# Identity products on an idle TensorE, pooled attention by two head pairs, and output tiles in a shared ring

## The chip, the cores and the metric

The kernel runs on one core of a Trainium2 chip. The metric is the device time of one execution in microseconds (us), the median of several executions. TensorE (PE) multiplies matrices into PSUM, its weight loads are counted as PEld; VectorE (DVE), ScalarE (ACT) and GpSimd (POOL) work element by element, POOL on SBUF only; SyncE (SP) issues the transfers. All engines take their queues in order.

## The reference, cut to what matters

Four sequences of 576 tokens, 8 heads of 64. Two attentions are added, one over means of four tokens, one over a band of seven, and a bilinear MLP follows.

```python
q_d = q.reshape(B, H, Sd, 4, D).mean(axis=3)        # the same for k and v, Sd = 144
out_d = sm_attn(q_d, k_d, v_d)                       # softmax(scale q k^T) v
out_up = np.repeat(out_d, 4, axis=2)
mask = np.abs(pos[:, None] - pos[None, :]) < 4
scores = np.where(mask, scale * np.matmul(q, k.transpose(0, 1, 3, 2)), -1000000000.0)
out_local = np.matmul(softmax(scores), v)
x = (out_up + out_local).transpose(0, 2, 1, 3).reshape(2304, 512)
result = ((x @ w_a) * (x @ w_b)) @ w_out             # w_a, w_b: 512 x 1536, w_out: 1536 x 512
```

## The kernel before, in words

**Tiling.** The 2304 tokens are cut in 9 units of 256 for the attentions and in 6 token tiles of 384 for the MLP. Heads go in 4 pairs (`NP`). The MLP splits each operand into a high and a low part (`xh`, `xl`; `gh`, `gl`; two halves of each `w`) and forms three products per pair of operands (`products`, lines 754 to 759). Per token tile there are 12 steps `f`, each with a product group `psa`, a group `psb` and a group `po`, 12 matmuls of 384 columns each, so 36 groups per token tile (`m_up`, `m_down`, lines 761 to 788). Afterwards `m_store` (lines 790 to 805) copies four PSUM banks to SBUF tiles `o` and stores them. For the first five token tiles the `o` tiles have a tag of their own with one buffer; for the last one they go to the tag `prod`, a ring of 3 buffers that the banded attention's products (`pr`, `av`) and the dense blocks' loads (`qk`, `vb`) use too.

**Weights.** 18 transfers of 1 MB bring the weights as 8-byte words; `w_pair` (lines 392 to 425) takes them apart: scalings and shifts on `ws`, a joining step to `wd`, the high part `w`, the low part `w`.

**Pooled attention.** For unit `u` and head pair `p`: `g_load` loads, `g_pools` sums four tokens (`g_sum`, lines 623 to 631, on POOL in three additions or on DVE in one reduction) into `qd`, `kd` and `vd`; `g_scores` (lines 649 to 667) multiplies into the bank `gs`, takes the negative maximum (`gnb`), exponentiates on ACT into `ge` with the sum in `gsm`; `g_norm` (669 to 674) divides; `g_turn` (676 to 685) transposes twice into `gt` and copies back; `g_out` (687 to 702) multiplies into `go` and copies to `xd`. `qd` has two buffers, one for odd and one for even pairs, and the banks come from the tag `misc` with two buffers. A unit that crosses two sequences has its products in two parts.

**Local attention.** The first two units (512 tokens, 8 blocks of 64) do it densely on PE (`d_steps`, lines 521 to 586: `ds` scores with a bf16 product of `band` that puts the mask in, `dt` transposes, `do` outputs, `add` adds the pooled part and splits into `xh`, `xl`). Blocks 0 to 5 make up the first token tile. The other seven units do it with products on POOL or DVE (`pr`, `av`), reductions on DVE (`sc`, `xloc`) and transposes on PE (`xp`); `x_steps` (lines 720 to 749) adds the pooled part and splits.

**What sets the order.** Nothing is issued as the functions are called: each call records a step with the engines that could do it, a cost for each, a rank and its predecessors. `Steps.order` (lines 202 to 268) then plans all engines by a list schedule in which the earliest possible step of the smallest rank goes first, `run_pe` (270 to 281) models PE's clock, and `emit` issues the result, which is fixed from then on. Ranks come from due times: `pooled`, `dense`, `banded` (lines 813 to 841) and the weights' line (857) take them from the constants of lines 46 to 62 (`PLAN`, `LEAD`, `LOAD_LEAD`, `W_STREAM`); the constants named `..._ON_DVE` are penalties for doing a step on DVE rather than on POOL or ACT. The prices of a step on PE stand in its call (0.174 us for an MLP product, 0.11 for a transpose of the pooled part, 0.06 for a dense output product).

Of the kernel before, what the change touches and what calls it, by code (L numbers as in the profile page):

```python
# [7 lines left out]
F32 = mybir.dt.float32  # L8
# [6 lines left out]
ALU = mybir.AluOpType  # L15
# [4 lines left out]
P = 128  # L20
# [37 lines left out]
LEAD = {"L": 2.852, "G": -12.651, "D0": -16.602, "D1": -2.24, "G0": 8.66}  # L58
PLAN = {"g0": -58.062, "g0s": 1.06, "g1": -27.374, "g1s": 4.983, "g2": 20.007, "g2s": 1.791,
        "d0": -31.319, "d0s": 5.13, "a0": -17.442, "a1": -7.9, "d1": 3.872, "d1s": 4.978, "t2": 19.293,  # L60
        "c2": 0.454, "t3": 34.824, "c3": 0.572, "t4": 57.774, "c4": 0.45, "t": -35.57, "c": 0.155}
LOAD_LEAD = {"L": -3.486, "G": 5.822, "D0": 13.151, "D1": -3.246, "G0": 20.908}
# [64 lines left out]
class Steps:  # L127
# [11 lines left out]
    def __init__(self, engines):  # L139
        self.engines, self.steps, self.tags = engines, [], {}  # L140
        self.rank, self.open = 0.0, None

# [59 lines left out]
    def order(self, window):  # L202
# [17 lines left out]
        done, duty = [], {}  # L220
        while True:
# [24 lines left out]
            if best is None:  # L246
                break
            at, e, (_, _, s, cost, _) = best
# [18 lines left out]
        assert len(done) == len(self.steps)  # L267
# [24 lines left out]
def tile_pooled_and_banded_attention__then__bilinear_mlp(  # L292
# [228 lines left out]
    def d_steps(b):  # L521
# [55 lines left out]
        def add():  # L577

            assert ready.count(u) == NP
# [53 lines left out]
    def g_pools(u, p):  # L633
# [8 lines left out]
        if b is not None:  # L642
            kd_t[b, p] = kd = tile_([P, NG], F32, "kd", f"kd{b}_{p}", bufs=5)
            vd_t[b, p] = vd = tile_([KC, 2, P], F32, "vd", f"vd{b}_{p}", bufs=5)
# [4 lines left out]
    def g_scores(u, p):  # L649
        qd = qd_t[p % 2].rearrange("p g j -> p (g j)")  # L650
        nb = tile_([P, 1], F32, "gnb", f"gnb{u}_{p}", bufs=2)
        tl = tile_([P, 2 * P], F32, "ge", f"ge{u}_{p}")
        e = tl[:, :NG]
        sm = tile_([P, 1], F32, "gsm", f"gsm{u}_{p}", bufs=2)
        ps = misc(f"gs{u}_{p}")[:, :NG]
# [11 lines left out]
        g_st[u, p] = (e, sm, tl)  # L667

    def g_norm(u, p):
        e, sm, _ = g_st[u, p]  # L670
        dve("tensor_scalar", 1, sm, sm, 1e-9, 4.0, op0=ALU.add, op1=ALU.mult)
        steps.steps[-1].shared = False
        dve("reciprocal", 1, sm, sm)
        act(NG, e, e, AF.Copy, scale=sm)

    def g_turn(u, p):
        e, _, tl = g_st[u, p]
        ps = misc(f"gt{u}_{p}")[:KC, : 2 * P]
# [6 lines left out]
        g_st[u, p] = pt.rearrange("p (c g j) -> p c g j", c=2, j=2)  # L685

    def g_out(u, p):
        pt = g_st.pop((u, p))
        ps = misc(f"go{u}_{p}")[:, :GU]
        steps.group()  # L690
        for n, (b, c0, c1) in enumerate(spans(u)):
            for c in range(2):

                for j in range(2):
                    rows = slice(j * D, (j + 1) * D)
                    mm(0.08, ps[rows, c0:c1], vd_t[b, p][:, c, rows], pt[:, c, c0:c1, j],
                       n == 0 and c == 0, c == 1, (c1 - c0) * KC / 6e2 / P)
# [3 lines left out]
        copy(GU, xd[u].part(p)[:, p], ps)  # L701
# [18 lines left out]
    def x_steps(u, th):  # L720
# [11 lines left out]
        def add():  # L732
            assert ready.count(u) == NP
# [56 lines left out]
    def m_store(m):  # L790
# [3 lines left out]
        for i, ps in enumerate(m_st["out"]):  # L794
            o = tile_([P, MT], F32, *(("prod", f"o{m}_{i}", 3) if m == NM - 1 else ("o", f"o{m}_{i}")))
# [70 lines left out]
    load(170, band, band_d)  # L866
    load(128, ident, ident_d)
    for t in qd_t:
# [4 lines left out]
    for m in range(NM):  # L873
# [6 lines left out]
        for s, (kind, f) in enumerate(slots):  # L880
# [4 lines left out]
            else:  # L885
                m_up(m, f, kind)
        steps.rank = m * 36 + 36
# [105 lines left out]
```

## Time and profile before

| | |
|---|---|
| median of 3 executions | 587.44 us (587.41 to 588.31) |
| the profiled execution | 586.48 us |
| its span, first to last instruction | 584.3 us |
| busy of the span: PE, DVE, ACT, POOL | 546.1, 407.0, 189.4, 277.2 us |
| chain that ended last, by engine | PE 87%, DVE 6%, DMA 3%, ACT 2% |
| mean granted TensorE clock | 0.998 |

How to read it: one execution was taken by the hardware profiler. An engine's busy time is the union of its instructions; a matmul's end is modelled and overlaps the next one's start, so the distance from start to start says more of PE than a duration. The chain follows back from the last instruction to what released each step. The granted clock is the share of TensorE's 2.4 GHz that the profiler's records show. In a row, `out<-in` names the tiles written and read, `x12` counts instructions, and `[0.92 <-DVE xl]` is the engine's idle time before the row and what ended it. All instructions stand at line 288, where `emit` issues them, so rows are told apart by tile.

### The profile page before, as it was taken

The page shows a single profiled execution, that of the slowest core. Times are in us where ns is not written, and L with a number is a line of the kernel's source. Part 1 is how long each engine was busy: PE and PEld are TensorE (multiplying, and loading weights), DVE is VectorE, ACT ScalarE, POOL GpSimd, SP SyncE. Part 2 cuts the span into 40 slices and gives each one's busy share as a digit, 9 for nine tenths or more (in the row PEclk, how much of TensorE's full clock was granted, in tenths as well). Part 3 has the DMA queues.
Part 4 walks back from the last instruction along what each step waited for, and adds up shares of the span by engine and source line. Part 5 has one row for each costly group of instructions (what it writes and reads, how often), then busy time and mean ns, then how long its engine had stood idle before and what let it go on. Part 6 is the DMA issues. An engine that isn't in the chain of part 4 may idle for free.

```text
span 584.3 us, 9037 instructions
## 1 busy us (share of the span) xinstructions
PE 546.1 (93%) x3432; PEld 517.9 (89%) x3432; DVE 407.0 (70%) x717; ACT 189.4 (32%) x464; POOL 277.2 (47%) x254
## 2 busy tenths in 40 slices
PE   2687599999989999999999999999999999999995
PEld 1565499889989999989999999999999999999995
DVE  5599999588989998888798897993787351221121
ACT  1599996222233123243212222231132111111111
POOL 4420421578867868769868696794154000000000
PEclk9999999999999999999999999999999999999999
DMA  8999990242133223422222432201110000000001
GB/s 235 343 360 375 345 320 2 85 151 72 72 110 102 76 79 102 145 87 103 70 82 64 153 96 78 82 32 50 33 42 13 2 1 0 28 28 0 1 1 54
DMA packets 22219, 59.51 MB, mean 102 GB/s; under 512 B 2544, under 2 KB 9072, under 8 KB 19872
## 3 DMA queue, kind: packets, MB, share of 16 engines
q1 hardware_dynamic: 22176, 58.93, 29.9%
q8 instruction: 27, 0.44, 0.3%
q14 instruction: 16, 0.13, 0.1%
HBM read 54.20 MB, written 4.72 MB: 101 GB/s over the span
## 4 chain that ended last, share of the span: by engine, by line
PE 87%; DVE 6%; DMA 3%; ACT 2%; issue 1%; SPq 0%; POOL 0%; ACTq 0%; DVEq 0%; POOLq 0%
PE psa L288 26%; PE psb L288 26%; PE po L288 24%; PE gs L288 3%; PE go L288 3%; DMA qk<-in_qk_dram 2%; PE ds L288 1%; PE gt L288 1%; DVE w L288 1%; DVE xloc L288 1%; PE dt L288 1%; PE do L288 1%; PE xp L288 1%; DVE xp L288 1%; DMA kv<-in_kqg_dram 1%
## 5 line engine op out<-in xcount | busy, mean ns | idle before, releaser
L288 PE MATMUL psa<-xh,w 128*128 128x384 f32 x576 | 162.5, 343 | 0.3 <-ACT xh L288 0.3
L288 PE MATMUL psb<-xh,w 128*128 128x384 f32 x576 | 160.7, 339 | 0.4 <-ACT a L288 0.4
L288 PE MATMUL po<-gh,w 128*128 128x384 f32 x576 | 160.0, 339 | 0.0
L288 POOL TENSOR_TENSOR pr<-q,k 128x896 f32<-128x896 f32 x50 | 106.3, 2146 | 7.4 <-DVE sc L288 2.3
L288 PEld LDWEIGHTS psa<-xh,w 128*128 128x128 f32 x576 | 106.2, 190 | 1.8 <-issue 1.1
L288 PEld LDWEIGHTS psb<-xh,w 128*128 128x128 f32 x576 | 105.4, 188 | 1.9 <-ACT a L288 0.6
L288 POOL TENSOR_TENSOR av<-v,sc 128x896 f32<-128x896 f32 x51 | 89.3, 1776 | 36.9 <-issue 17.8
L288 PEld LDWEIGHTS po<-gh,w 128*128 128x128 f32 x576 | 105.1, 188 | 1.0 <-issue 0.9
L288 DVE TENSOR_TENSOR psb<-psb,a 128x384 f32<-128x384 f32 x72 | 40.4, 561 | 93.7 <-PE psb L288 92.6
L288 DVE TENSOR_REDUCE xloc<-av 128x128 f32<-128x896 f32 x56 | 98.3, 1770 | 5.3 <-POOL av L288 5.2
L288 PE MATMUL psa<-xl,w 128*128 128x384 f32 x288 | 97.2, 337 | 0.9 <-DVE xl L288 0.9
L288 PE MATMUL psb<-xl,w 128*128 128x384 f32 x288 | 96.6, 335 | 0.0
L288 PE MATMUL po<-gl,w 128*128 128x384 f32 x288 | 96.5, 335 | 0.0
L288 ACT ACTIVATE gh<-psb 128x384 fp32r<-128x384 f32 x72 | 35.4, 491 | 119.9 <-DVE psb L288 116.9
L288 ACT ACTIVATE a<-psa 128x384 f32<-128x384 f32 x72 | 35.3, 490 | 119.1 <-PE psa L288 118.6
L288 DVE TENSOR_REDUCE sc<-pr 128x14 f32<-128x896 f32 x56 | 59.4, 1077 | 3.1 <-POOL pr L288 2.9
L288 PEld LDWEIGHTS psa<-xl,w 128*128 128x128 f32 x288 | 54.7, 190 | 1.2 <-DVE xl L288 1.2
L288 PEld LDWEIGHTS psb<-xl,w 128*128 128x128 f32 x288 | 54.3, 188 | 0.0
L288 PEld LDWEIGHTS po<-gl,w 128*128 128x128 f32 x288 | 54.1, 188 | 0.1
L288 DVE TENSOR_TENSOR gl<-psb,gh 128x384 fp32r<-128x384 f32 x72 | 39.6, 550 | 17.3 <-ACT gh L288 17.3
L288 ACT ACTIVATE ws<-ws 128x1024 f32<-128x1024 f32 (+1 forms) x35 | 38.3, 1141 | 0.0
L288 PE MATMUL gs<-kd,qd 128*128 128x144 f32 (+2 forms) x96 | 25.0, 354 | 9.4 <-DVE kd L288 8.2
(86 smaller groups left out, 527.1 us busy)
## 6 DMA issues: line engine op xcount, KB each, us to landing
ws<-in_w_dram SPq DMA_DIRECT2D x18, 1024.0 KB
k<-in_kl_dram SPq DMA_DIRECT2D x14, 448.0 KB
v<-in_vl_dram SPq DMA_DIRECT2D x14, 448.0 KB
kq<-in_kqg_dram SPq DMA_DIRECT2D x12, 416.0 KB
q<-in_ql_dram SPq DMA_DIRECT2D x14, 256.0 KB
vr<-in_vg_dram SPq DMA_DIRECT2D x12, 288.0 KB
qk<-in_qk_dram SPq DMA_DIRECT2D x8, 396.0 KB
out_dram<-o SPq DMA_DIRECT2D x24, 128.0 KB
```

The lines of the kernel that those rows point to most:

```text
L288: getattr(self.engines[s.engine], op)(real(out), *map(real, args), **{k: real(v) for k, v in kw.items()})
```

## The change

- `order` puts *spare* steps on PE: from the end of the load of `band` until the first MLP group is planned, whenever PE's planned free time is before the next step of any engine, a product of a 128 x 128 bf16 identity (the last columns of `band`) with itself is put in, priced at 0.06 us, into the bank `po3`, which nothing reads.
- `g_scores`, `g_norm`, `g_turn` and `g_out` work on two head pairs: their products stand in one bank side by side, maxima, small scalings, reciprocals and copies are done once at twice the width, and exponentials and divisions on ACT stay one per pair. They are planned at the odd pairs' times. `ge` is twice as large, `gnb` has one buffer rather than two, `kd` and `vd` have six rather than five.
- All `o` tiles go to the ring `prod`.
- The planner's constants have new values.

```diff
-ON_DVE = 1.868
-COPY_ON_DVE = 4.816
-SCALE_ON_DVE = -0.32
-FITS = 0.299
-PATIENCE = {"DVE": 0.292, "ACT": 0.222}
-W_STREAM = (-7.851, 0.732, -8.289)
-W_LEAD, W_STEP = 62.416, 1.671
-EAGER = 0.728
-POOLS_ON_DVE = 2.555
-SIGN_ON_DVE = 2.712
-HI_ON_DVE = -0.497
-LO_ON_DVE = -51.032
-LEAD = {"L": 2.852, "G": -12.651, "D0": -16.602, "D1": -2.24, "G0": 8.66}
...
+ON_DVE = 15.452
+COPY_ON_DVE = 5.43
+SCALE_ON_DVE = 4.078
+FITS = 0.311
+PATIENCE = {"DVE": 0.297, "ACT": 0.029}
+W_STREAM = (-4.856, 1.136, -12.242)
+W_LEAD, W_STEP = 56.213, 1.509
+EAGER = 0.662
+POOLS_ON_DVE = 7.049
+SIGN_ON_DVE = 5.126
+HI_ON_DVE = -6.133
+LO_ON_DVE = -16.529
+LEAD = {"L": 4.681, "G": -10.577, "D0": -7.099, "D1": 1.827, "G0": -9.485}
...
@@ order
+            if warm and free["PE"] < best[0] - 0.05 * (best[1] == "PE"):
+
+                x = Step(0.0)
+                x.ways, x.engine = {"PE": self.spare}, "PE"
+                x.start, x.end = free["PE"], self.run_pe(free["PE"], self.spare[0], 1.0, duty)
+                free["PE"] = x.end
+                done.append(x)
+                spares += 1
+                continue
...
+            if s is self.spare_from:
+                warm = True
+                free["PE"] = max(free["PE"], s.end + self.LANDING)
+            if s is self.spare_to:
+                warm = False
@@ g_scores
-        ps = misc(f"gs{u}_{p}")[:, :NG]
+        ps = misc(f"gs{u}_{pp}")[:, : 2 * NG]
...
-        for n, (b, c0, c1) in enumerate(parts):
-            rows = slice(2 * c0, 2 * c1) if n else slice(0, P)
-            mm(0.27, ps[rows], qd[:, rows], kd_t[b, p], True, True)
+        for i in range(2):
+            qd = qd_t[i].rearrange("p g j -> p (g j)")
+            for n, (b, c0, c1) in enumerate(parts):
+                rows = slice(2 * c0, 2 * c1) if n else slice(0, P)
+                mm(0.27, ps[rows, i * NG : (i + 1) * NG], qd[:, rows], kd_t[b, 2 * pp + i], True, True)
         steps.close()
-        dve("tensor_reduce", NG, nb, ps, axis=AX.X, op=ALU.max)
-        dve("tensor_scalar", 1, nb, nb, -1.0 / 128, None, op0=ALU.mult)
+        dve("tensor_reduce", 2 * NG, nb, ps.rearrange("p (i g) -> p i g", i=2), axis=AX.X, op=ALU.max)
+        dve("tensor_scalar", 2, nb, nb, -1.0 / 128, None, op0=ALU.mult)
         steps.steps[-1].shared = False
-        act(NG, e, ps, AF.Exp, bias=nb, scale=1.0 / 128, accum_out=sm)
+        for i in range(2):
+            act(NG, tl.part(i)[:, i, :NG], ps[:, i * NG : (i + 1) * NG], AF.Exp, bias=nb[:, i : i + 1],
+                scale=1.0 / 128, accum_out=sm.part(i)[:, i : i + 1])
@@ g_turn
-        for c in range(2):
-            turn(0.11, ps[:, c * P : (c + 1) * P], e[:, c * KC : (c + 1) * KC], ident)
+        for i in range(2):
+            for c in range(2):
+                turn(0.11, ps[:, (2 * i + c) * P : (2 * i + c + 1) * P], tl[:, i, c * KC : (c + 1) * KC], ident)
         steps.close()
         pt = tl[:KC]
-        copy(2 * P, pt, ps)
+        copy(4 * P, pt, ps.rearrange("p (i n) -> p i n", i=2))
@@ g_out
-        copy(GU, xd[u].part(p)[:, p], ps)
+        copy(2 * GU, xd[u].part(pp)[:, 2 * pp : 2 * pp + 2], ps)
@@ m_store
-            o = tile_([P, MT], F32, *(("prod", f"o{m}_{i}", 3) if m == NM - 1 else ("o", f"o{m}_{i}")))
+            o = tile_([P, MT], F32, "prod", f"o{m}_{i}", 3)
@@ pooled
-            for dt, f in ((0.1, g_pools), (0.45, g_scores), (0.75, g_norm), (0.9, g_turn), (1.05, g_out)):
-                at(tp + dt * step, stream, lambda f=f, p=p: f(u, p))
+            at(tp + 0.1 * step, stream, lambda p=p: g_pools(u, p))
+            if p % 2:
+                for dt, f in ((0.45, g_scores), (0.75, g_norm), (0.9, g_turn), (1.05, g_out)):
+                    at(tp + dt * step, stream, lambda f=f, p=p: f(u, p // 2))
...
     load(170, band, band_d)
+    steps.spare_from = steps.steps[-1]
     load(128, ident, ident_d)
+    idle = bank("po3", "idle")[:, :P]
+    unit = band[:, 3 * KB :]
+    steps.group()
+    mm(0.06, idle, unit, unit, True, True)
+    steps.close()
+    steps.spare = steps.steps[-1].ways["PE"]
...
                 m_up(m, f, kind)
+            steps.spare_to = steps.spare_to or steps.steps[-2]
```

## Rows read from the trace of the kernel before

**Rows 1.** Windows, all engines; busy us with instruction counts, granted clock, DMA share.

```profile
core 0: us, PE busy (x) PEld busy (x) DVE busy (x) ACT busy (x) POOL busy (x), PEclk, DMA share, GB/s
0.00:16.60 16.60, 3.17 (x15) 1.79 (x15) 9.46 (x20) 3.02 (x7) 7.53 (x15) 1.00 0.88 243
16.60:48.00 31.40, 23.93 (x157) 18.54 (x158) 22.75 (x59) 24.50 (x73) 8.83 (x17) 1.00 0.95 354
48.00:71.80 23.80, 15.79 (x113) 12.59 (x112) 23.36 (x38) 23.55 (x56) 6.51 (x7) 1.00 1.00 364
100.00:160.00 60.00, 60.00 (x409) 56.66 (x408) 46.86 (x77) 15.41 (x40) 43.08 (x36) 1.00 0.28 93
```

**Rows 2.** Chain that ended last, 16.6 to 48 us, then 48 to 72.2 us, shares.

```profile
by line: DMA qk<-in_qk_dram 35.0%; PE ds L288 24.4%; PE do L288 10.1%; PE dt L288 9.4%; PE gs L288 7.5%; PE go L288 6.4%; DVE w L288 5.8%; issue 4.3%; DVE gnb L288 4.2%; ACT ge L288 4.1%; DVE ge L288 4.0%; PE gt L288 3.9%; DVE wd L288 3.6%;
...
by line: DVE w L288 21.7%; ACT ws L288 10.0%; DVE wd L288 9.8%; DVE vd L288 7.9%; ACT dw L288 7.4%; ACT w L288 6.1%; issue 5.1%; PE dt L288 4.4%; ACT ge L288 4.4%; DVE do L288 4.3%; PE go L288 3.0%; POOL dw L288 2.7%; DVE dw L288 2.5%; ACT 
```

**Rows 3.** The same chain in order of time, the first MLP products (start, us).

```profile
72.19 3.84 PE psa L288 x12
76.03 2.37 PE psb L288 x12
78.40 2.08 PE psa L288 x12
```

**Rows 4.** Timeline of PE (start, us), before and after the first product.

```profile
62.20 1.82 PE L288 MATMUL ds<-qk 128*128 128x70 f32 x8
...
81.03 0.30 PE L288 MATMUL ds<-band 128*128 128x280 bf16 x1
81.17 1.00 PE L288 MATMUL ds<-qk 128*128 128x70 f32 x8
...
102.89 0.60 PE L288 MATMUL dt<-ident,dw 128*70 128x128 f32 x4
103.24 0.42 PE L288 MATMUL po<-gh,w 128*128 128x384 f32 x1
```

**Rows 5.** Timeline of PE, inserted groups between MLP products.

```profile
105.53 0.69 PE L288 MATMUL do<-dw,vb 70*64 70x64 f32 x16
...
167.56 0.46 PE L288 MATMUL go<-ge,vd 72*64 72x64 f32 x8
167.94 0.51 PE L288 MATMUL gs<-kd,qd 128*128 128x144 f32 x2
168.20 0.43 PE L288 MATMUL psa<-xh,w 128*128 128x384 f32 x1
...
315.28 0.38 PE L288 MATMUL gt<-ident,ge 128*72 128x128 f32 x2
315.42 0.42 PE L288 MATMUL psb<-xh,w 128*128 128x384 f32 x1
315.68 0.34 PE L288 MATMUL psb<-xl,w 128*128 128x384 f32 x1
```

**Rows 6.** DVE groups of the whole span: count, busy us, mean ns, idle before.

```profile
L288 DVE TENSOR_REDUCE gnb<-gs 128x1 f32<-128x144 f32 x36 | 10.8, 301 | 8.8 <-PE gs L288 8.5
L288 DVE COPY ge<-gt 72x256 f32<-72x256 f32 x13 | 5.4, 419 | 5.7 <-PE gt L288 5.4
L288 DVE TENSOR_SCALAR gnb<-gnb 128x1 f32<-128x1 f32 x36 | 5.5, 154 | 1.2
L288 DVE TENSOR_REDUCE dnb<-ds 128x4 f32<-128x280 f32 x8 | 3.5, 440 | 2.5 <-PE ds L288 2.5
L288 DVE COPY dw<-dt 70x512 f32<-70x512 f32 x2 | 1.4, 681 | 0.4 <-PE dt L288 0.4
```

**Rows 7.** Timeline of PE at the starts of the second and third token tile.

```profile
163.15 0.44 PE L288 MATMUL psa<-xl,w 128*128 128x384 f32 x1 [0.92 <-DVE xl L288]
...
252.92 0.48 PE L288 MATMUL gs<-kd,qd 128*128 128x144 f32 x2 [0.57 <-DVE xl L288]
```

**Rows 8.** Timeline of all engines at the end of the program.

```profile
580.38 0.56 DVE L288 COPY o<-po 128x384 f32<-128x384 f32 x1 [3.39 <-DMA out_dram<-o]
```

More of the change, by code (lines that the diff above doesn't have):

```diff
@@ L141, in __init__ @@
         self.rank, self.open = 0.0, None
+        self.spare, self.spare_from, self.spare_to = None, None, None
     def tile(self, pool, shape, dtype, tag, name, bufs=1):
@@ L219, in order @@
                 add(s)
-        done, duty = [], {}
+        done, duty, warm, spares = [], {}, False, 0
         while True:
@@ L266, in order @@
                     add(n)
-        assert len(done) == len(self.steps)
+        assert len(done) - spares == len(self.steps)
         return sorted(done, key=lambda s: s.start)
@@ L577, in add @@
         def add():
-            assert ready.count(u) == NP
+            assert ready.count(u) == NP // 2
             ps = st["x"]
@@ L642, in g_pools @@
         if b is not None:
-            kd_t[b, p] = kd = tile_([P, NG], F32, "kd", f"kd{b}_{p}", bufs=5)
-            vd_t[b, p] = vd = tile_([KC, 2, P], F32, "vd", f"vd{b}_{p}", bufs=5)
+            kd_t[b, p] = kd = tile_([P, NG], F32, "kd", f"kd{b}_{p}", bufs=6)
+            vd_t[b, p] = vd = tile_([KC, 2, P], F32, "vd", f"vd{b}_{p}", bufs=6)
             g_sum(NG, [(kd, slice(0, P))], kq[:, : 4 * NG].rearrange("p (r g) -> p r g", r=4))
@@ L647, in g_pools, with g_scores @@
                   vr[:KC].rearrange("p (r d) -> p r d", r=4))
[L649 to L654, printed above, removed]
-        ps = misc(f"gs{u}_{p}")[:, :NG]
+    def g_scores(u, pp):
+        nb = tile_([P, 2], F32, "gnb", f"gnb{u}_{pp}")
+        tl = tile_([P, 2, 2 * P], F32, "ge", f"ge{u}_{pp}")
+        sm = tile_([P, 2], F32, "gsm", f"gsm{u}_{pp}", bufs=2)
+        ps = misc(f"gs{u}_{pp}")[:, : 2 * NG]
@@ L676, in g_turn, with g_norm @@
-    def g_turn(u, p):
-        e, _, tl = g_st[u, p]
-        ps = misc(f"gt{u}_{p}")[:KC, : 2 * P]
+        for i in range(2):
+            act(NG, tl.part(i)[:, i, :NG], ps[:, i * NG : (i + 1) * NG], AF.Exp, bias=nb[:, i : i + 1],
+                scale=1.0 / 128, accum_out=sm.part(i)[:, i : i + 1])
+        g_st[u, pp] = (sm, tl)
+    def g_norm(u, pp):
+        sm, tl = g_st[u, pp]
+        dve("tensor_scalar", 2, sm, sm, 1e-9, 4.0, op0=ALU.add, op1=ALU.mult)
+        steps.steps[-1].shared = False
+        dve("reciprocal", 2, sm, sm)
+        for i in range(2):
+            e = tl.part(i)[:, i, :NG]
+            act(NG, e, e, AF.Copy, scale=sm[:, i : i + 1])
@@ L679, in g_turn @@
+    def g_turn(u, pp):
+        _, tl = g_st[u, pp]
+        ps = misc(f"gt{u}_{pp}")[:KC]
         steps.group()
-        for c in range(2):
-            turn(0.11, ps[:, c * P : (c + 1) * P], e[:, c * KC : (c + 1) * KC], ident)
+        for i in range(2):
+            for c in range(2):
+                turn(0.11, ps[:, (2 * i + c) * P : (2 * i + c + 1) * P], tl[:, i, c * KC : (c + 1) * KC], ident)
         steps.close()
         pt = tl[:KC]
-        copy(2 * P, pt, ps)
-        g_st[u, p] = pt.rearrange("p (c g j) -> p c g j", c=2, j=2)
@@ L687, in g_out @@
-    def g_out(u, p):
-        pt = g_st.pop((u, p))
-        ps = misc(f"go{u}_{p}")[:, :GU]
-        steps.group()
[L691 to L697, printed above, removed]
+        copy(4 * P, pt, ps.rearrange("p (i n) -> p i n", i=2))
@@ new lines, in g_turn, with g_out @@
+        g_st[u, pp] = pt.rearrange("p i (c g j) -> p i c g j", c=2, j=2)
+    def g_out(u, pp):
+        pt = g_st.pop((u, pp))
+        ps = misc(f"go{u}_{pp}")[:, : 2 * GU].rearrange("p (i g) -> p i g", i=2)
+        steps.group()
+        for i in range(2):
+            for n, (b, c0, c1) in enumerate(spans(u)):
+                for c in range(2):
+                    for j in range(2):
+                        rows = slice(j * D, (j + 1) * D)
+                        mm(0.08, ps[rows, i, c0:c1], vd_t[b, 2 * pp + i][:, c, rows], pt[:, i, c, c0:c1, j],
+                           n == 0 and c == 0, c == 1, (c1 - c0) * KC / 6e2 / P)
@@ L732, in add @@
         def add():
-            assert ready.count(u) == NP
+            assert ready.count(u) == NP // 2
             up = xd[u].rearrange("p k (c t r) -> p k t r c", t=2, r=1)[:, :, th]
```

14 lines of the change are left out of this document (4 added, 10 removed).

## The prediction

> **What bounds the kernel now.** I read the windows first. From 100 to 160 us PE is busy 60.00 of 60 us [rows 1]: once the MLP runs, TensorE sets the time. So the end is the moment of the first MLP product, plus PE's work after it, plus PE's few stalls. The timeline of PE shows the stalls: the second token tile waits 0.92 us at 163.15 for `xl`, the third one 0.57 us at 252.92 [rows 7]. Short as they are, they say that `x` arrives just in time there.
>
> Before 71.8 us no engine is the bound alone. From 16.6 to 48 us PE, DVE and ACT are each busy for 23 to 25 of 31.4 us, and the chain lies on PE for 24.4 + 10.1 + 9.4 + 7.5 + 6.4 + 3.9 = 61.7% of the stretch, 19.4 us (the transfer's 35.0% reaches back before it). From 48 us on DVE is busy 23.36 and ACT 23.55 of 23.8 us [rows 1], and the chain lies on weight decoding, `w`, `ws` and `wd`, for 47.6%, 11.3 us; PE has only 4.4 + 3.0% [rows 2].
>
> Is TensorE slow there? The granted clock reads 1.00 in every window [rows 1], yet eight `ds` products take 1.82 us at 62.20 and 1.00 us at 81.17 [rows 4], and the first twelve MLP products take 3.84 us, the next 2.37, later ones 2.08 [rows 3]. 3.84/12 = 0.320 us for 384 columns is 1.2 columns a nanosecond; 2.08/12 = 0.173 us makes it 2.2, near 2.4. I go by the durations: PE is at the lower level, 1.2 GHz, until about 76 us, having idled between short groups until then.
>
> **Part 1, the fillers: the first products.** With PE kept busy the first 24 products should last 2 x 2.08 instead of 3.84 + 2.37: 2.05 us off the path; I take 2.0 (from 0, if the clock isn't up, to 2.05).
>
> **Part 1: the stage before.** `ds` goes to 1.00/1.82 = 0.55 of its time. Of 19.4 + 0.074 x 24.2 = 21.2 us of PE on the chain, 0.45 could go: 9.5 us at most, and nothing at least if DVE and ACT step into the hole. What is late next is those two: after 48 us both are full. But half of that chain is weight decoding that the first product doesn't need beyond its first pair, and the new priorities decode later pairs later; PE needs a pair for every two of its 2.08 us slots. I take 7 us, nearer the top, because the first stretch has 31.4 - 22.75 = 8.65 us of DVE idle into which work can move. More sums go to POOL (busy 6.51 of 23.8 us), such as the `vd` reduction, 7.9% of the second stretch, 1.9 us [rows 1, 2].
>
> **Part 1: the price of a filler.** A filler is one weight load and one 128-column bf16 product. The planner puts them wherever its own model sees PE idle and prices them at 0.06 us; on the chip PE takes its queue in order, so what they take beyond that delays every product queued behind them, and DVE and ACT wait for those. Real work before the first product: 3.17 + 23.93 + 15.79 = 42.9 us slow, 23.6 us fast. With the first product at 64 us and fillers from about 5 us on, 64 - 5 - 23.6 = 35 us are left, some 590 fillers. The nearest row is the bf16 product with the same stationary, 280 columns, which holds PE from 81.03 to 81.17 us, 0.14 us: by columns 0.064 us. The far bound is an fp32 transpose, 128 columns too: four and their leaving take 102.89 to 103.24, 0.35 us, 0.09 each, and two more of them add 0.60 - 0.38 = 0.22 us, 0.11 each [rows 4, 5]. Below, 0.053 (128 columns at 2.4 GHz) would leave PE waiting a little, without loss. I take 0.063: 590 x 0.003 = 1.8 us lost; from 0 to 590 x 0.05 = 30 us.
>
> The Trainium skill, TensorE: Matmul & The Clock Gate, section Back-to-back issue gap, speaks against the change: it says that a sustained stream of load and product pairs with 128 columns runs at about 81 ns each. By that the term would be 590 x 0.021 = 12.4 us. No row here shows such a stream in bf16.
>
> **Part 2, two head pairs at once.** On DVE and ACT two of everything become one of twice the width. Nearest rows: a reduction over 144 takes 301 ns, over 280 440; the small scalings 154 ns whatever the width; a 256-wide copy 419, a 512-wide one 681 [rows 6]. Two score maxima 602 to 440, the two small steps behind exp and maximum 2 x 154 saved, two copies 838 to 681: some 0.6 us per merge, 0.9 with the reciprocal and the output copy at the same rate. The exps and scalings on ACT stay two. Four merges before the first product: 3 us of DVE and ACT; I count 1 us of it, since the chain is only partly there.
>
> On PE, after the first product, 28 pair steps become 14. Output: sixteen products last 0.69 us, eight 0.46: +0.23 for eight more, against 0.38 us from the second group's start to what follows it: 0.15 saved. Transposes: two hold PE for 0.14 us (315.28 to 315.42), four for 0.35: 0.07 lost. Scores: two hold it 0.26 us (167.94 to 168.20); four cost at most twice that: nothing saved. And the first product after a group stays 0.26 us instead of 0.17 (315.42 to 315.68): 28 such exits fewer x 0.09 = 2.5 us [rows 3, 4, 5]. Sum 14 x 0.08 + 2.5 = 3.6; I take 3 (0 to 5, as the planner may split groups or put them side by side as now).
>
> Both `qd` buffers now serve one step, so POOL's next `qd` sums wait for the pair's score group, and POOL's products queue behind them. POOL is idle for 17 of 60 us between 100 and 160 [rows 1], which hides it; without that cover it delays `x`, counted below. The sixth `kd`/`vd` buffer only lets loads start sooner.
>
> **Part 3, output tiles in the ring.** Four output tiles for each of the first five token tiles no longer wait for one buffer, but hold ring slots that POOL's and DVE's products want. A copy waited 3.39 us for a landing at the end, where the ring is already used [rows 8]. The cover is again POOL's idle time; SP's queue holds the same stores, in order with the loads of q, k and v behind them. I take nothing; up to 3 us if it falls on a late `x`. The tail is unchanged.
>
> **The new constants** reorder every engine and SP's queue. What they do on the path is the start above and the stalls. The second and third tiles' `x` must now come 8 us sooner: DVE has 60 - 46.86 = 13.1 us idle between 100 and 160 [rows 1], the merges give up to 0.9 us each for six and ten merges, but decoding moved behind the first product takes back about 8. I take 2 us more stall (0 to 8).
>
> **Sum.** The profiled execution took 586.5 us (span 584.3, and 2.2 around it), 1.0 under the median of 587.4. 586.5 - 7 - 1 - 2 - 3 + 1.8 + 2 = 577.3; with the 1.0 of the median, 578.3 us.
>
> **Rivals.** *`x` is the bound.* If the supply of `x` for the third tile stays where it is, the start's gain turns into stalls before 252.9 us: left are its 0.6 us stall and eight merges after it, 8 x 0.2 = 1.6: about 585.3. For it: both tiles wait now [rows 7]. Against it: DVE's 13.1 idle us and the merges. 0.2.
>
> *Fillers cost too much,* the rival on the slow side. PE becomes the bound before the first product, since all of its time there is planned full. It decides from where 590 times the excess eats the other 11 us: 79 ns a filler. At 94 ns, midway from there to the bound of 110, it costs 590 x 0.034 = 20 us: 586.5 - 11 + 20 + 1 = 596; 606 at the bound. For it: no row has such a stream. Against it: the bf16 row, and that the planner's other prices for PE fit the rows (0.174 for an MLP product, 0.11 for a transpose). By the Trainium skill's 81 ns (the section named above) it would be 589. 0.18.
>
> *It doesn't warm anything.* Taking the granted clock of 1.00 at its word, there is nothing to warm; then the merges remain, 586.5 - 3 + 1 + up to 2 of stall: 586. Against it: the doubled durations. 0.05.
>
> **How the numbers follow.** The forecast has 0.57; its own range is 571 to 584 (start 3 to 10 us sooner, stalls 0 to 4, groups 1 to 5). The 8 in 10 range takes in the `x` rival and the mildest overrun of fillers: 570 to 589. About 0.2% can be told from no change, 1.2 us. Faster: 0.57 and most of the `x` rival, 0.73. Same: 0.08, from the edges of both and the third rival. Slower: 0.19, the fillers and a little of stalls that outgrow the gain.
>
> **What would show it.** First `psa` near 66 us, twelve in 2.08 us; `ds` x8 near 1.00 us at 20 us; fillers 0.056 to 0.064 us from start to start. Wrong: a first `psa` after 72 us with PE never idle before it (fillers), or a stall of several us for `xl` at the second or third tile (`x`), or first products at 3.84 us still.

## The result and the profile after

| | before | after |
|---|---|---|
| median | 588.16 us (587.41 to 589.34, 6 runs) | 592.02 us (590.40 to 594.27, 6 runs) |
| ratio to before | | 1.0066, 95% interval 1.0039 to 1.0094 |
| profiled execution, its span | 586.48, 584.3 us | 592.62, 590.8 us |
| first MLP product of `psa` | 71.84 us | 65.21 us |
| TensorE from there to its last product | 506.11 us | 519.22 us |

The forecast was 578.3 us, the result is 0.66% slower than before. The start came 6.6 us sooner, near the 6.2 of the sum (7 + 1 - 1.8). What followed took 13.1 us more. The two windows that reach from TensorE's first MLP product to its last one say of what kind these are. Of before:

```profile
71.84:577.95 506.11, 503.12 (x3151) 484.92 (x3149) 350.87 (x602) 138.19 (x330) 254.30 (x216) 1.00 0.21 69
```

and of after, with three of the windows that stand in [rows 1] ahead of it:

```profile
0.00:16.60 16.60, 12.12 (x154) 11.57 (x155) 9.25 (x12) 3.37 (x8) 8.87 (x21) 1.00 0.88 258
16.60:48.00 31.40, 30.18 (x473) 28.12 (x471) 23.56 (x52) 25.49 (x80) 7.86 (x15) 1.00 0.92 334
100.00:160.00 60.00, 56.22 (x381) 51.72 (x380) 50.56 (x74) 14.61 (x37) 38.95 (x31) 1.00 0.24 80
...
65.21:584.43 519.22, 503.18 (x3166) 484.37 (x3163) 371.07 (x544) 140.94 (x334) 251.31 (x209) 1.00 0.23 73
```

The columns are those of [rows 1]: length, then busy PE, PEld, DVE, ACT, POOL. PE is busy for 503.1 us in both; its idle time grew from 506.11 - 503.12 = 3.0 to 519.22 - 503.18 = 16.0 us. From 100 to 160 us, where nothing was idle before, 3.8 us are. And DVE has fewer instructions (544 for 602) but 20.2 us more to do. Who PE waits for, from 65 us on, is told by the list of waits (total us, times, longest):

```profile
PE psb L303 <- DVE gl L303: 5.8, 6, 1.8
PE xp L303 <- DVE xloc L303: 3.2, 4, 1.2
PE gt L303 <- ACT ge L303: 2.5, 3, 1.2
...
PE dt L303 <- DVE dw L303: 1.9, 1, 1.9
...
PE psa L303 <- DVE xl L303: 1.3, 2, 1.0
```

All but one name DVE, and `ge` on ACT waits for DVE's `gnb` and `gsm` in its turn (26.3 and 12.3 us in all). There is no one large wait for `xl`, which the prediction had named as the sign of trouble, but a score of small ones for work of all kinds: DVE is late throughout. The chain says the same by engine: before it was PE 87% and DVE 6%, after it is

```profile
PE 53%; DVE 18%; issue 2%; POOL 1%; ACT 0%; DMA 0%; SPq 0%; DVEq 0%; ACTq 0%
```

These are shares of the whole span, and the chain after could be followed back to 142.9 us only. From 148 to 577 us, which both chains cover, DVE has 3% before and 25% after.

What made DVE late stands in its groups, by shape (count, busy us, mean ns):

```profile
L303 DVE TENSOR_TENSOR pr<-q,k 128x896 f32<-128x896 f32 x6 | 13.5, 2243 | 0.0
L303 DVE TENSOR_SCALAR gsm<-gsm 128x2 f32<-128x2 f32 x18 | 11.9, 662 | 3.7 <-ACT ge L303 3.6
L303 DVE TENSOR_SCALAR gnb<-gnb 128x2 f32<-128x2 f32 x18 | 9.7, 536 | 0.6
L303 DVE TENSOR_TENSOR av<-v,sc 128x896 f32<-128x896 f32 x8 | 8.7, 1092 | 0.3
...
L303 DVE RECIPROCAL gsm<-gsm 128x2 f32<-128x2 f32 x18 | 3.0, 166 | 0.6
```

A scaling of one number per partition took 154 ns [rows 6], a scaling of two takes 536 and 662 on average, about four times as long; the reciprocal of the same two numbers takes 166. One of them can be followed in the chain of waits (start, us, what):

```profile
280.37 1.11 DVE xloc L303
281.47 0.52 issue
281.99 0.55 DVE psb L303
282.54 2.04 DVE gsm L303
284.58 0.02 issue
284.60 0.17 DVE gsm L303
284.77 1.62 DVE xloc L303
286.39 0.48 DVE gl L303
286.87 0.04 issue
286.91 2.37 PE psb L303 x12
```

`gsm` holds DVE for 2.04 us, the reciprocal and the reduction `xloc` queue behind it, `gl` comes after them, and PE waits for `gl` (0.86 us idle at 286.91). What POOL does at that moment, in its timeline:

```profile
282.39 2.15 POOL L303 TENSOR_TENSOR pr<-q,k 128x896 f32<-128x896 f32 x1
```

POOL's product ends at 284.54 us and DVE's scaling, issued at 282.46 by DVE's timeline with 2.11 us, at 284.57. The scaling did not work for 2 us, it waited for POOL.

### The profile page after: what moved, and what is told of

Its sections match the earlier page's. It is cut to its first block, busy times and chain, and to the rows that moved or that the text cites. A ratio compares the mean times of both kernels' runs of the same rounds, so it can differ in the third digit from the quotient of the medians.

```text
span 590.8 us, 10186 instructions
## 1 busy us (share of the span) xinstructions
PE 562.1 (95%) x4070; PEld 540.2 (91%) x4070; DVE 420.7 (71%) x629; ACT 186.6 (32%) x452; POOL 268.0 (45%) x245
## 4 chain that ended last, share of the span: by engine, by line
PE 53%; DVE 18%; issue 2%; POOL 1%; ACT 0%; DMA 0%; SPq 0%; DVEq 0%; ACTq 0%
PE psb L303 18%; PE psa L303 16%; PE po L303 15%; DVE xloc L303 6%; DVE sc L303 3%; DVE pr L303 1%; DVE gnb L303 1%; DVE psb L303 1%; DVE gl L303 1%; DVE gsm L303 1%; PE go L303 1%; DVE xp L303 1%; PE gs L303 1%; POOL av L303 1%; DVE av L303 1%
## 5 line engine op out<-in xcount | busy, mean ns | idle before, releaser
L303 PE MATMUL psa<-xh,w 128*128 128x384 f32 x576 | 160.0, 338 | 0.0
L303 POOL TENSOR_TENSOR pr<-q,k 128x896 f32<-128x896 f32 x50 | 106.3, 2150 | 21.4 <-DMA out_dram<-o 13.4
L303 POOL TENSOR_TENSOR av<-v,sc 128x896 f32<-128x896 f32 x48 | 85.9, 1815 | 44.2 <-issue 26.3
L303 PE MATMUL idle<-band 128*128 128x128 bf16 x638 | 41.2, 226 | 2.7 <-DMA band<-in_band_dram 2.7
L303 PEld LDWEIGHTS <-band 128*128 128x128 bf16 x646 | 39.8, 102 | 3.5 <-DMA band<-in_band_dram 2.7
```

The lines of the kernel that those rows point to most:

```text
L303: getattr(self.engines[s.engine], op)(real(out), *map(real, args), **{k: real(v) for k, v in kw.items()})
```

## The experiments

The reading to be tested: **a scaling two elements wide cannot run beside POOL's products, and the lateness it brings makes DVE's own products meet POOL's as well.** Two products meet when DVE's starts while one of POOL's runs, and takes longer by it. The rivals: the output tiles in the ring (POOL waits 13.4 us in two pieces for stores to free a `pr` buffer), the new constants, and an early start that turns into stalls whatever is done, because the middle of the kernel can deliver no sooner. In all of them but e2_told, e5_fill_only and e6_oldconst the order of instructions on every engine is that of the kernel named (e4_before_wide, e7_apart, e9_both, e10_before_apart and e11_apart_nofill have memsets in between).

| run | kernel | median us | ratio to before, 95% | first `psa` | PE idle after it |
|---|---|---|---|---|---|
| | before | 588.16 | | 71.8 | 3.0 |
| | after | 592.02 | 1.0066 (1.0039 to 1.0094) | 65.2 | 16.0 |
| e1_split | after, scalings one element wide | 585.27 | 0.9964 (0.9939 to 0.9988) | 63.2 | 10.2 |
| e2_told | after, planner told of the wait | 599.87 | 1.0230 (1.0198 to 1.0262) | 71.3 | 17.8 |
| e3_nofill | after, no identity products | 604.95 | 1.0325 (1.0292 to 1.0358) | 75.8 | 14.3 |
| e4_before_wide | before, scalings two elements wide | 602.89 | 1.0276 (1.0253 to 1.0299) | 73.7 | 14.0 |
| e5_fill_only | before and identity products alone | 591.24 | 1.0074 (1.0041 to 1.0107) | 65.8 | 14.6 |
| e6_oldconst | e1_split, constants of before | 600.73 | 1.0219 (1.0173 to 1.0265) | 56.7 | 24.8 |
| e7_apart | e1_split, POOL kept off DVE's products | 580.19 | 0.9875 (0.9845 to 0.9905) | 63.6 | 7.3 |
| e8_tail | e1_split, last output tile elsewhere | 583.96 | 0.9938 (0.9912 to 0.9963) | 64.7 | 12.4 |
| e9_both | e7_apart and e8_tail | 579.79 | 0.9859 (0.9830 to 0.9887) | 65.4 | 6.6 |
| e10_before_apart | before, POOL kept off DVE's products | 588.51 | 1.0014 (0.9997 to 1.0032) | 72.0 | 3.1 |
| e11_apart_nofill | e7_apart, no identity products | 590.45 | 1.0051 (1.0033 to 1.0068) | 74.4 | 4.9 |

Idle times are the sums of TensorE's idle marks behind that product, in the profiled execution of each. That execution lies 3.2 us below the median in e1_split (582.04 us) and 3.2 to 3.3 above it in e2_told, e5_fill_only and e8_tail (603.15, 594.41, 587.15), so the idle times say less than the medians. Ratios are to runs of before on the same chip.

**e1_split: the width alone.** Every two-element scaling becomes two of one element. The plan still counts one step.

```diff
+    def halves(op, t, *a, **k):
+        steps.group()
+        for i in range(2):
+            o = t[:, i : i + 1]
+            steps([("DVE", 0.03604, 0.0, op, (o, *a), k)], o)
+        steps.close()
...
-        dve("tensor_scalar", 2, nb, nb, -1.0 / 128, None, op0=ALU.mult)
+        halves("tensor_scalar", nb, -1.0 / 128, None, op0=ALU.mult)
```

> The changed kernel with each two-element scaling of gnb and gsm issued as two one-element ones; the planned order of every engine is the same, step by step. Theory A (port): a two-element scaling on DVE waits until POOL's running instruction ends, a one-element one does not; the 36 scalings took 21.6 us instead of about 6, and DVE's lag spreads. Then no scaling is over 0.2 us, the idle time of PE after the first MLP product falls from 16 to 4 to 8 us, and the time from 592 to 577 to 583. Theory B (supply): x cannot come sooner whatever the start gains; 588 to 592. Theory C (ring): POOL waits for output stores (13.4 us) and everything behind is late; 588 to 592.

Two instructions for one, and the time falls by 6.7 us (592.02 to 585.27 by the medians; the two intervals don't touch). No scaling takes over 0.16 us, as expected; the time and PE's idle time of 10.2 us stay above what was expected of them (577 to 583 us, 4 to 8 us). In its groups on DVE:

```profile
L303 DVE TENSOR_TENSOR pr<-q,k 128x896 f32<-128x896 f32 x6 | 14.9, 2488 | 0.0
L303 DVE TENSOR_TENSOR av<-v,sc 128x896 f32<-128x896 f32 x8 | 11.5, 1436 | 0.8 <-DVE sc L303 0.6
...
L303 DVE TENSOR_SCALAR gsm<-gsm 128x1 f32<-128x1 f32 x36 | 4.4, 147 | 2.6 <-ACT ge L303 2.3
L303 DVE TENSOR_SCALAR gnb<-gnb 128x1 f32<-128x1 f32 x36 | 3.9, 149 | 0.6
```

The scalings are down from 21.6 to 8.3 us together. The products of DVE are not: fourteen take 26.4 us, against 22.2 in the changed kernel and 7.3 + 6.4 for eleven of them before. So the width is one cause, and something is left. The second half of the reading fails here: with the scalings short, the products meet as they do in the changed kernel, so it is not the scalings' lateness that makes them meet. They do it in the changed kernel's order; why there is not traced.

**e4_before_wide: the width put into the kernel before.** The scaled number gets a second, unused one beside it; nothing else moves.

```diff
-        dve("tensor_scalar", 1, nb, nb, -1.0 / 128, None, op0=ALU.mult)
+        dve("tensor_scalar", 1, nb2, nb2, -1.0 / 128, None, op0=ALU.mult)
...
-        dve("tensor_scalar", 1, sm, sm, 1e-9, 4.0, op0=ALU.add, op1=ALU.mult)
+        dve("tensor_scalar", 1, sm2, sm2, 1e-9, 4.0, op0=ALU.add, op1=ALU.mult)
```

> The kernel before with its scalings of gnb and gsm made two elements wide (the second column is a constant that nothing uses), the planned order the same but for four small memsets on POOL. Theory A: many of the 72 scalings now wait for POOL, 10 to 25 us of DVE in all, and the time goes from 588 to 594 to 604. Theories B and C: the scalings are as short as before, 587 to 589.

One more element in 72 instructions costs 2.8%. But for four memsets on POOL at the start, the instructions, their order and the transfers are the same; PE's idle time goes from 3.0 to 14.0 us:

```profile
L288 DVE TENSOR_SCALAR gnb<-gnb 128x2 f32<-128x2 f32 x36 | 24.4, 677 | 1.2
...
L288 DVE TENSOR_SCALAR gsm<-gsm 128x2 f32<-128x2 f32 x36 | 19.8, 550 | 4.8 <-ACT ge L288 4.0
```

That is 44.2 us where [rows 6] has 5.5 for `gnb` and the same view 5.4 for `gsm`: 33.3 us more, above the 10 to 25 expected, while the time is in its range (594 to 604). One scaling waited for the product of POOL that was running and for the two behind it, on DVE and then on POOL:

```profile
274.96 4.41 DVE L288 TENSOR_SCALAR gnb<-gnb 128x2 f32<-128x2 f32 x1
...
274.36 4.98 POOL L288 TENSOR_TENSOR av<-v,sc 128x896 f32<-128x896 f32 x3
```

With e1_split, the price of the width is shown from both sides. DVE's eleven products take 13.2 us here and 13.7 before: in this order, late scalings bring no more meetings.

**e2_told: let the planner avoid it.** The flag that says a scaling doesn't share anything with POOL goes.

```diff
-        steps.steps[-1].shared = False
...
-        steps.steps[-1].shared = False
```

> The changed kernel with the planner told that the two-element scalings share POOL's port, so that it plans POOL and DVE apart there; every engine's order changes after the first ones. Theory A: scalings over 0.4 us become rare, and the time is 580 to 590, worse than with one-element scalings because the planner now keeps POOL away. Theories B and C: 588 to 594.

It got worse, and no theory on record had that (594 us at most). The scalings still take 10.7 and 8.5 us in all, since a plan sets the order on each engine and not the moment: nothing in the kernel keeps the two apart as it runs. The plan that results is another one (first `psa` at 71.3 us, 689 identity products), so this run says that telling the planner is no cure; it says nothing on the size of the wait.

**e3_nofill: the identity products' worth.** They are planned and not issued.

```diff
+            if hasattr(s, "spare"):
+                continue
```

> The changed kernel without its 637 filler products, the planned order of all else the same. The first MLP products should last 3.8 and 2.4 us again and the first one start 5 to 9 us later, at 70 to 74 us, if the fillers are what brought it to 65.2. Theory A: DVE is what lags after the start, so that part of the delay is taken up by fewer stalls on PE: 593 to 598. Theory B: the end is set by x, so it stays: 591 to 593. Theory C says nothing of the start: 598 to 601, the whole delay.

The first product comes 10.6 us later than in the changed kernel and the time is 12.9 us longer, with PE's idle time about the same (14.3 us). That is more than any theory on record allowed (601 at most): the whole delay and 2.3 us. The 2.3 are in the first products: 24 of them take 6.89 us here and 4.41 after. And here the record shows the lower of TensorE's two levels, 1.2 GHz, in the stretch before them, a granted clock (third number from the end) of 0.50 where the changed kernel has 1.00:

```profile
48.00:75.80 27.80, 11.20 (x95) 9.50 (x95) 23.27 (x35) 25.29 (x52) 4.35 (x5) 0.50 0.94 348
```

So the identity products do what they are meant to. Without them the first product comes 3.9 us later than before the change (75.8 for 71.8): all of the 6.6 us by which the start is sooner is theirs, in an order that was planned with them. What is lost is lost elsewhere.

**e5_fill_only and e6_oldconst: is an early start enough?** The first adds the identity products to the kernel before, with its constants, and nothing else of the change (the hunks in `order` and those around `spare`). The second takes e1_split back to the constants of before (the hunk of lines 46 to 62).

> The kernel before with the fillers alone: one head pair at a time, one-element scalings, a buffer of its own for the output tiles, its own constants; the planner orders all engines anew around the faster start. Theory S (start): the first MLP product sets the end, it comes 8 to 11 us sooner, and the time is 576 to 580. Theory X (x): DVE and POOL deliver x for the second tile no sooner under these constants, PE waits there instead, at 155 to 165 us, and the time is 584 to 592.

> The changed kernel with one-element scalings and all planner constants of the kernel before. Theory S: the first product sets the end; it comes at 55 to 60 us, so the time is 570 to 580. Theory X: weights and x come late instead, PE's idle time after the first product is 20 us and more, and the time is 588 to 602.

The identity products alone bring the first product from 71.8 to 65.8 us, and the second token tile starts at 168.5 instead of 161.8 us: 12.7 us are lost in between, 11.0 of them as more idle time of PE. After three waits of 0.98 to 1.29 us between 156 and 160.4 us its clock is at the lower level, and the waits go on:

```profile
161.20:171.40 10.20, 4.82 (x14) 3.42 (x15) 9.79 (x21) 3.22 (x8) 7.06 (x4) 0.50 0.44 144
```

Two transposes `xp` take 0.69 us at 162.04 for 0.41 at 160.32. e6_oldconst has 0.50 from 155.8 to 166.0 us and 0.77 on average from 370 to 392. So PE's waits cost more there than their idle marks. With the old constants the first product comes at 56.7 us, the earliest of all, and the time is among the longest, with 24.8 us of idle PE. In these two an early start by itself is worth nothing: what must come next has to come early too. So the new constants are a part of the change that pays; with them and narrow scalings it is 585.27, without them 600.73 us (the old ones belong to the kernel before).

**e7_apart: no meeting of products.** In e1_split, DVE's products of 896 columns take up to 5.15 us. In the changed kernel one such meeting reads, on DVE and then on POOL:

```profile
183.31 4.98 DVE L303 TENSOR_TENSOR pr<-q,k 128x896 f32<-128x896 f32 x1
...
183.14 2.13 POOL L303 TENSOR_TENSOR pr<-q,k 128x896 f32<-128x896 f32 x1
...
185.22 2.12 POOL L303 TENSOR_TENSOR pr<-q,k 128x896 f32<-128x896 f32 x1
```

The planner keeps DVE's products and POOL's apart in its plan. On the chip POOL had started its own 0.17 us before DVE's here. The edit makes POOL wait for each DVE product or weight difference that stands ahead of POOL's next step in the plan, by a one-column memset on either engine:

```diff
+            if held and s.engine == "POOL":
+                self.engines["POOL"].memset(real(self.token), 0.0)
+                held = False
...
+            if s.engine == "DVE" and len(s.ways) == 2 and s.shared and s.ways["DVE"][0] > 0.9 and "POOL" in s.ways:
+                self.engines["DVE"].memset(real(self.token), 0.0)
+                held = True
```

It also puts the dense blocks' `dnb` into the two buffers of `mx`; this part has no run of its own.

> The kernel with one-element scalings (planned order kept), in which POOL's next instruction waits for a DVE product or weight difference that the plan puts ahead of it (a one-element memset on each side carries the wait). In the run with one-element scalings six DVE products lasted 2.3 to 5.2 us instead of 1.1, as POOL had started first. Theory A (port): none is over 1.5 us now, PE idles 2 to 6 us less, 579 to 584 against 585.3. Rival: POOL is as late as DVE was, or the memsets cost more than they save; 584 to 590.

580.19 us, 0.9875 of before, 5.1 us below e1_split, and no product of DVE over 1.5 us (the longest takes 1.45), as expected. Its DVE groups:

```profile
L307 DVE TENSOR_TENSOR av<-v,sc 128x896 f32<-128x896 f32 x8 | 8.7, 1092 | 0.3
L307 DVE TENSOR_TENSOR pr<-q,k 128x896 f32<-128x896 f32 x6 | 6.9, 1150 | 0.0
...
L307 DVE TENSOR_SCALAR gsm<-gsm 128x1 f32<-128x1 f32 x36 | 4.5, 145 | 2.8 <-ACT ge L307 2.5
L307 DVE TENSOR_SCALAR gnb<-gnb 128x1 f32<-128x1 f32 x36 | 3.9, 148 | 0.6
```

Scalings and products of DVE together: 43.8 us after, 34.7 in e1_split, 24.0 here. POOL pays for it by 18 small memsets, before which it sits idle for 99.3 us in all, but these waits stand in place of others: it is busy 260.4 of 578.8 us here and 268.0 of 590.8 after. Its wait for `out_dram`, 13.4 us after and 13.5 in e1_split, is no longer in its list of waits, but POOL waits for DVE in the same places instead: 11.73 us at 423.00, where e1_split has 9.73 at 422.02, and 5.37 at 335.65 for 3.79 at 334.40. So what e7_apart gains is not POOL's standing still there. PE's row of the window from first to last MLP product now reads

```profile
63.61:572.39 508.78, 501.48 (x3166) 486.14 (x3163) 353.32 (x595) 142.73 (x335) 243.54 (x225) 1.00 0.23 74
```

with 17.8 us less of DVE than after, 7.3 us of idle PE and the last product 12.0 us sooner.

**e10_before_apart: do these waits help any kernel?** The same edit in the kernel before.

> The kernel before, with the one part that separates e7_apart from e1_split: POOL waits for the DVE products and weight differences that stand ahead of its own in the order. Theory (collisions of DVE and POOL products grow out of DVE being late, and the kernel before had three of them, about 2.2 us over the usual duration of a product together): 585 to 588 us, no more than 2 us faster. Rival (the waits help whatever the kernel, and account for e7_apart alone): about 5 us faster, 582 to 584, as e7_apart stood to e1_split; then the change itself is worth only some 2 us.

No change that can be told (0.9997 to 1.0032), half a microsecond above what the theory gave. The products of DVE fall to 1113 and 1090 ns on average, from 1220 and 1273, and PE's idle time stays where it was: before the change DVE had room for its few meetings. The rival, that the waits are a gain whatever the kernel, falls; they mend what the changed order had made.

**e11_apart_nofill: the early start, once the middle keeps up.** e7_apart without issuing the identity products.

> e7_apart without issuing the identity products, order and everything else kept. Theory (with the collisions gone, a late first product passes to the end whole): first product of the first pooled attention 7 to 12 us later than e7_apart's 63.6, and the time as much later, 587 to 593 us. Rival (the middle has slack of its own that takes up a late start, as a kernel bound by DVE would): first product as late, time under 585 us.

First product 10.8 us later than in e7_apart, the time 10.3 us longer. The whole of the start reaches the end here, while in e5_fill_only nothing of 6 us did. But it did so in the changed kernel too (e3_nofill: 10.6 us and 12.9), with the meetings in. So the theory's condition, that the meetings must be gone, is not what decides. What these two orders have, and e5_fill_only and e6_oldconst have not, are the new constants.

**e8_tail and e9_both: the last wait for the ring.** The last output tile gets room of the tile `k`, which is done by then.

```diff
+            if (m, i) == (NM - 1, NP - 1):
+                o.buf.args = (sb, [P, (TC + 6) * D], F32, "k", 1, f"o{m}_{i}")
```

> The kernel with one-element scalings (planned order kept), the last of the 24 output tiles in the room of the banded attention's k, which is free by then, rather than in the ring of three. The last copy waited 3.4 us for the first store there. If the ring costs that at the end: 1.5 to 3 us off, 582 to 584. If the last stores are bound by the transfers alone: 585.3 as before.

> The kernel of e7_apart with the last output tile in k's room as in e8_tail; the order is the same. Theory (the end is the last token tile's transfer and not its wait for a buffer, and the waits of POOL are what e7_apart already took out): the last copy no longer waits for out_dram, the time is 579 to 580.5 us, at most 0.7 us from e7_apart's 580.19. Rival (the ring's stores still delay work in mid-kernel, and the freed buffer lets it run on): 577 us or less.

The last copy no longer waits for a store, as DVE's last rows show, those of after first, then those of e9_both:

```profile
586.85 0.56 DVE L303 COPY o<-po 128x384 f32<-128x384 f32 x1 [3.43 <-DMA out_dram<-o]
```

```profile
573.36 0.56 DVE L307 COPY o<-po 128x384 f32<-128x384 f32 x1 [1.02 <-PE po L307]
```

The copy comes 2.4 us sooner after its predecessors, and the end only about half a microsecond: from PE's last product to the end of the span it is 6.4 us after and 5.8 in e9_both, because the store that follows takes its time: the last copy of e9_both is done at 573.92 us and the span ends 5.2 us later. e8_tail against e1_split (583.96, 585.27) and e9_both against e7_apart (579.79, 580.19) are no differences that these runs can tell. e9_both has the lowest median of all.

**Not tried:** the ring alone. No run has the new order with output tiles in a buffer of their own, nor the ring without the rest. What there is against it as a cause: in e1_split POOL waits 13.5 us for stores as in the changed kernel, and the time fell by 6.7 us all the same; in e7_apart and e9_both the ring is in, POOL stands still in the same places, and the time is the lowest. A small part of the loss can still be the ring's.

## Why the prediction was wrong, point by point

**The step that failed** is in part 2: "the small scalings 154 ns whatever the width". [rows 6] has one width only, 128x1; the sentence read a second width into it. The wide ones take 157 to 170 ns when POOL is idle and up to 2107 when it is not. There was a sign in the kernel: the flag `shared`, set to `False` behind each of these scalings, tells the planner that they, unlike other steps of DVE, need not be kept apart from POOL's; the change left it so at twice the width. And what was at hand could have bounded the price: POOL is busy 43.08 of 60 us in the MLP [rows 1], with products of about 2.15 us, so a scaling that has to wait for POOL waits half a product seven times in ten, 0.77 us on average by this estimate, and 28 scalings after the first product come to some 22 us of DVE. Measured over all 36: 21.6 us for what was costed at 36 x 0.154 = 5.5, so 16 us of waiting, and taking it out was worth 6.7 us of time (e1_split). The bound from above was missing, and the gain of "some 0.6 us per merge" was booked without it.

The Trainium skill has the rule. SBUF — State Buffer, section Who interferes with whom, says that VectorE shares one pair of SBUF ports with GpSimd, that `tensor_scalar` in a two-port mode takes that pair, and that of two instructions wanting it the later one blocks until the first is finished; VectorE: DVE Perf Modes, section What auto-detection actually checks, gives as its conditions a single source, source and destination in SBUF, and outermost dimensions (those of length 1 left aside) that are both even or equal. Two elements are even. The traces agree: the scaling issued at 282.46 us ends 0.03 us after POOL's product, `tensor_reduce` never shows such a wait (`gnb` over 288 columns takes 434 to 458 ns in after, e1_split and e7_apart). The traces go further in one point: a product of DVE and a scaling also waited for products of POOL queued behind the running one (4.98 us at 183.31 after, 4.41 us in e4_before_wide). Of a single element that section says nothing; the traces show that it doesn't wait. Weighed before the result, this rule would have been the rival on the slow side.

**The second failed step** is the term of stalls, "I take 2 us more stall (0 to 8)", and its cover, that DVE's 13.1 idle us between 100 and 160 cover what moves there. The term measured +13.0 us. e1_split and e7_apart part it: by idle time of PE 16.0, 10.2 and 7.3, about 6 us go with the width and 3 with the meetings; by e8_tail, e1_split's kernel but for its last tile, with 12.4, it is 4 and 5. (After and e8_tail have an idle mark of 1.9 and 1.7 us for `dt` near 84 us that e1_split has not; there POOL waits 30 us for the load `kq`, 4 in e1_split.) By medians the width is worth 6.7 us and the meetings 5.1. About 4 us of idle time are left with the new order itself, near the 2 that were counted. Idle share was the wrong cover: DVE takes its work in order, and a few waits of 2 us delay whatever is planned right behind, `gl` and `xloc` above all, though its mean load stays at 71%.

**Not counted** was that one more dense block moved behind the first product: after has nine `ds` products at 71.73 us, beside the nine that before has there too, and four more `dt`,

```profile
71.73 0.30 PE L303 MATMUL ds<-band 128*128 128x280 bf16 x1
71.87 1.00 PE L303 MATMUL ds<-qk 128*128 128x70 f32 x8
72.92 0.44 PE L303 MATMUL psb<-xh,w 128*128 128x384 f32 x1
```

1.19 us for the first and 0.35 for a `dt` group, 1.5 us together.

**Right:** the first `psa` (forecast near 66, measured 65.21; by e3_nofill the identity products bring all of it, so nothing shows the 1 us that the sum had for merges ahead of it); eight `ds` products at 25.00 us in 1.00 us, against 1.82 at 62.20 before [rows 4]; the first products, in the timeline of PE,

```profile
65.21 0.42 PE L303 MATMUL psa<-xh,w 128*128 128x384 f32 x1
...
67.51 0.34 PE L303 MATMUL psb<-xh,w 128*128 128x384 f32 x1
...
69.62 0.33 PE L303 MATMUL psa<-xh,w 128*128 128x384 f32 x1
```

24 of them in 4.41 us, against 6.56 from the first `psa` at 71.84 to 78.40 before [rows 3], and without the identity products again 6.89 (e3_nofill); and the price of an identity product, 0.056 to 0.064 forecast:

```profile
46.34 4.58 PE L303 MATMUL idle<-band 128*128 128x128 bf16 x79
50.76 0.60 PE L303 MATMUL dt<-ident,dw 128*70 128x128 f32 x4
```

(50.76 - 46.34) / 79 = 0.056 us. There are 638. By that row the 81 ns of the Trainium skill (TensorE: Matmul & The Clock Gate, section Back-to-back issue gap) don't hold for this stream, and the rival "fillers cost too much" falls with e3_nofill and e11_apart_nofill. "It doesn't warm anything" falls by the `ds` row and by the granted clock of 0.50 in e3_nofill.

**PE's groups** were forecast at -3 us. From start to start, with the longer product behind each group, scores and outputs of two pairs take 0.22 to 0.26 us less as one step in e7_apart than as two before, and the transposes as long: some -0.25 us a merge, 14 merges, -3.5. This size was right. All the same PE's busy time after the first product is unchanged, 503.1 us, where -2.15 (first products) - 3.5 + 1.5 should have made it 499. In e1_split and e7_apart it is 500.5 and 501.5. A part of this is what a stall costs beyond its idle mark: the transposes at 285.41 hold PE until 286.91, 1.50 us, against 0.36 in e7_apart for the same group, so 1.14 us are lost where the mark says 0.86. There are 18 such marks over 0.15 us after and 6 before: some 3 us by this estimate. The rest isn't traced.

**The rival "`x` is the bound"** (585.3) was the nearest in kind: `xl` still comes late at the second token tile, 1.04 us for 0.92 [rows 7], and gains of the start are lost before 253 us (the second token tile starts 0.8 us sooner instead of 6.6, the third 3.5). But the loss goes on behind it: the fifth tile starts 6.0 us later than before.

With the waits taken out, the change comes to 579.79 us (e9_both), 1.5 from the forecast and inside its own range of 571 to 584. That nearness is in part luck. In the traces, e9_both's first product is 6.4 us sooner than before's, where the sum had 6.2, but from there to the last one it takes 1.8 us more (507.92 for 506.11), where the sum had 3 less (2 and 3 off, 2 on). PE is busy 1.8 us less than before there, for 5 in the sum, and waits 3.6 us more, for 2. By the profiled execution it is 3.6 us from the sum (580.94 for 577.3); the rest is that its median lies 1.2 us below that execution, where the forecast had it 1.0 above. So the start was right in size, PE's savings show at less than half of their sum, and what was missing is one price on DVE and the meetings of products.

## What to carry to other kernels

When two operations are merged into one of twice the width, ask for each whether the wider form still runs beside the engine next to it, and bound its price by that engine's longest instruction, not by the narrow form's duration (one scaling waited for three of them, in e4_before_wide). A plan that keeps two engines apart in time is only a plan: here products met in the new order, and waits put into the kernel were worth 5.1 us, but nothing in the order of before (e10_before_apart). An earlier start is worth its whole length or nothing, depending on whether the stages behind it can deliver earlier: identity products were worth 10.3 us in e7_apart, 12.9 in the changed kernel, and brought no gain in e5_fill_only.

## What the runs showed of the hardware that I had not expected

- `tensor_scalar` in place on 128x1 takes 101 to 160 ns whatever POOL does (before, e1_split, e7_apart); on 128x2 it takes 157 to 2107 ns after and up to 4408 in e4_before_wide, in most cases ending some 0.03 us after a product of POOL's. `reciprocal` on the same 128x2 takes 165 to 169 ns in after, e1_split and e7_apart. So an instruction split in two is the faster one here: 8.3 us for the 72 narrow scalings of e1_split, 21.6 for the 36 wide ones after.
- What waits for POOL does not always get in between two of its products that follow each other at once. The scaling at 282.46 us after did; the one at 274.96 in e4_before_wide let three pass, and the DVE product at 183.31 after let two pass (to 187.34 us) and then took its usual 1 us.
- A stream of identity products of 128 bf16 columns, each with its weight load, runs at 0.056 us each on TensorE (79 of them from 46.34 us on). Of the first 63, from 2.74 us on, some fifty took 0.107 us each and the rest 0.056; the granted clock reads 1.00 for all of it (0 to 16.6 us), so there the durations tell more than the record.
- TensorE's clock falls in mid-kernel too: in e5_fill_only the granted clock is 0.50 from 161.2 to 171.4 us, after three waits of 0.98, 1.12 and 1.29 us between 156 and 160.4.
